# Moving operands of the two networks' products at many SBUF offsets instead of one

## The chip, the cores and the metric

The kernel runs on one core of a Trainium2 chip. Its time is the device time of one execution in microseconds (us); the figure for a kernel is the median of its runs, so lower is better. TensorE's clock has two levels, 1.2 and 2.4 GHz; the profile gives it as a share of 2.4 GHz.

## The reference, cut to what matters

Windowed attention (4 batches, 8 heads, 576 positions, head size 64) gives 2304 tokens of 512 features. Two feed-forward networks follow, one after the other, each 512 to 2048 to 512:

```python
x = attention(q, k, v)                  # 2304 x 512
h = x @ moe_w_in                        # 2304 x 2048
g = np.maximum(h, 0.0) + alpha * np.minimum(h, 0.0)
x = g @ moe_w_out                       # 2304 x 512
h = x @ moe2_w_in
g = np.where(h >= 1, h, np.where(h <= -1, 0.0, (h + 1) ** 2 / 4.0))
return g @ moe2_w_out
```

## The kernel before, in words

**Work.** Features lie on the 128 partitions, tokens along the free axis. The tokens of a network (a phase, `ph`) are cut into five token tiles, four of 512 and one of 256: in the first network the narrow one is the fourth tile, in the second the fifth. For each token tile the kernel goes through 16 blocks `f` of 128 hidden features. One step of that walk (a slot) makes a block of `h` in `f_h`, its activation in `f_g`, and the share of `y` that an earlier block gives in `f_y`; `f_y` runs two slots behind `f_h`. The order on each engine is the order in which the code issues.

**Products.** Every fp32 operand is split into a high part and a remainder, both float32r, and three products are added up: low weights by high data, high weights by low data, high by high. A slot has 4 chunks of 128 features, so 12 products in `f_h` (L344 to L346) and 12 in `f_y` (L384 to L386). Each has a 128x128 stationary operand (the weights) that it loads itself and a moving operand of 512 or 256 columns. With 10 token tiles and 16 blocks that is 3840 products, 3072 of 512 columns and 768 of 256.

**Moving operands.** `f_h` reads `xh` and `xl`, which `x_split` writes once per token tile and chunk: ScalarE copies `X` to `xh` (L317), VectorE subtracts (L318). They come from the pool `xs_p` with four buffers each, one per chunk. `f_y` reads `gh` and `gl`, which `f_g` (ScalarE, L366) and `f_cut` (VectorE, L372; GpSimd for the first token tile) write. They come from the pool `g_p` with two buffers each, which alternate with `f`.

**Where things lie.** Each of these buffers is 2048 bytes in a partition, and `PAD` is a tile of 336 floats that no instruction touches, placed between the early pools and the late ones. In the program as built `xh` begins at byte 135328, `xl` at 143520, `gh` at 219296 and `gl` at 223392, and all twelve buffers begin at 160 modulo 2048, which is 32 modulo 128. The weights' tiles (`wih`, `wil`, `woh`, `wol`) are of 2048 bytes too and also begin at 160 modulo 2048; each product loads a 512-byte chunk of one.

**Around it.** Attention of the first batch runs ahead of the networks; that of the other three is issued between the products of the first network (`attention_point`). Weights are read by DMA, rebuilt by VectorE (`w_make`), and split by ScalarE and GpSimd (`w_cut`, `wo_split`).

Of the kernel before, what the change touches and what calls it, by code (L numbers as in the profile page):

```python
# [11 lines left out]
F32R = mybir.dt.float32r  # L12
# [10 lines left out]
P = 128  # L23
# [25 lines left out]
TW = 512  # L49
WARM = 10  # L50

PAD = 336
DS = D + 1

FIRST = (0, 2)
# [24 lines left out]
def attention_then_two_ffns(ctx: ExitStack, tc: tile.TileContext, a0, aqk, av, w1i, w1o, w2i, w2o, alpha, masks, ident, out):  # L80
# [5 lines left out]
    xs_p = ctx.enter_context(tc.tile_pool(name="xs_p", bufs=4))  # L86
# [5 lines left out]

    ctx.enter_context(tc.tile_pool(name="pad", bufs=1)).tile([P, PAD], F32, name="pad")
    X = [const.tile([P, NT], F32, name=f"X{c}") for c in range(NC)]
# [216 lines left out]
    def x_split(n, c, on_pool=False):  # L311
        ph, t = n
        t0, w = TILES[ph][t]
        hi = xs_p.tile([P, TW], F32R, tag="xh", name="xh")
        lo = xs_p.tile([P, TW], F32R, tag="xl", name="xl")
        src = X[c][:, t0:t0 + w]
        nc.scalar.activation(hi[:, :w], src, AF.Copy)  # L317
        (nc.gpsimd if on_pool else nc.vector).tensor_tensor(lo[:, :w], src, hi[:, :w].bitcast(F32), ALU.subtract)  # L318
        xt[n, c] = (hi, lo)
# [28 lines left out]
    def f_g(n, f, between):  # L348
        ph, t = n
        w = TILES[ph][t][1]  # L350
        ps = ht.pop((n, f))[:, :w]
        t = g_p.tile([P, TW], F32, tag="g", name="g")[:, :w]
        hi = g_p.tile([P, TW], F32R, tag="gh", name="gh")[:, :w]
        lo = g_p.tile([P, TW], F32R, tag="gl", name="gl")[:, :w]
        if ph == 0:

            nc.scalar.activation(t, ps, AF.Relu, scale=-1.0)  # L357
            between()
            nc.vector.scalar_tensor_tensor(t, t, al[:, f:f + 1], ps, ALU.mult, ALU.add)  # L359
            ps = t  # L360
        else:
            nc.vector.tensor_scalar(t, ps, 1.0, -1.0, ALU.min, ALU.max)  # L362
            nc.scalar.activation(t, t, AF.Square, bias=half, scale=0.5)  # L363
            between()
            nc.vector.tensor_tensor(ps, ps, t, ALU.max)  # L365
        nc.scalar.activation(hi, ps, AF.Copy)  # L366
        gt[n, f] = (hi, lo)
        return ps
# [37 lines left out]
    with tc.manual_schedule(), ExitStack() as late:  # L406
# [75 lines left out]
        for i in range(NGB):  # L482
            e_scores(i)
            if i >= 1:
                a_turn(i - 1, ps_a, "a")
            e_exp(i)
            if i >= 2:
                a_out(i - 2, ps_a, "w")
            else:
                fill(2)  # L490
            if i >= 1:
                e_values(i - 1)
            w_cut()
            if i in FIRST:
                conv(3)
            if i == 3:
                x_split(n0, 0, True)

                nc.gpsimd.memset(qk[0], 0.0)
                hold = False  # L500
                a_load_qk(NGB)
                w_load(*pend_l.pop(0))
                w_load(*pend_l.pop(0))
                a_load_v(NGB)
                more()
            if i == 4:
                x_split(n0, 1, True)
# [5 lines left out]
        conv(1)  # L513
        e_values(NGB - 1)
        x_split(n0, 2)
        f_h(n0, 0, (1,))
        f_h(n0, 1, (1,))
# [17 lines left out]
        g_p = late.enter_context(tc.tile_pool(name="g_p", bufs=2))  # L535
# [25 lines left out]
        for k in range(len(slots) + 2):  # L561
            n, f = slots[k] if k < len(slots) else (None, None)
# [13 lines left out]
            if n:  # L576
                if nn and f == NF - 1:
                    for c in range(NC):
                        x_split(nn, c)
                if k < 2:  # L580
                    ops = EARLY[k]
                elif n == n0:
                    ops = 6
                elif n == order[5] or (n == order[4] and 2 <= f < NF - 2):
                    ops = 3 + 3 * (f % 2)
                else:
                    ops = 0
                attention_point()
                b0, b1 = BEFORE[n[0]]
                g = f_g(n, f, lambda: conv(min(ops, b0)))  # L590
                ops -= min(ops, b0)
                first_ops = min(ops, b1) if k else 1
                conv(first_ops)
                f_cut(n, f, g)
                if k == 0:
                    wo_split(n, f)
                w_cut()
# [97 lines left out]
```

## Time and profile before

| | |
|---|---|
| median of 3 runs | 878.41 us (877.32 to 879.67) |
| span of the profiled execution, first to last instruction | 875.2 us |
| mean granted TensorE clock | 0.994 |
| TensorE busy | 859.9 us, 98% of the span |
| VectorE, ScalarE, GpSimd busy | 53%, 43%, 32% |

The profile records only the span of its execution, not that execution's own device time; the median of the runs is 3.2 us above the span. PE is TensorE's matmul, PEld its weight load, DVE VectorE, ACT ScalarE, POOL GpSimd, SP SyncE. A matmul's end is modelled and matmuls overlap in the record, so the pace of a row of products is read from their starts.

### The profile page before, as it was taken

The page shows a single profiled execution, that of the slowest core. Times are in us where ns is not written, and L with a number is a line of the kernel's source. Part 1 is how long each engine was busy: PE and PEld are TensorE (multiplying, and loading weights), DVE is VectorE, ACT ScalarE, POOL GpSimd, SP SyncE. Part 2 cuts the span into 40 slices and gives each one's busy share as a digit, 9 for nine tenths or more (in the row PEclk, how much of TensorE's full clock was granted, in tenths as well). Part 3 has the DMA queues.
Part 4 walks back from the last instruction along what each step waited for, and adds up shares of the span by engine and source line. Part 5 has one row for each costly group of instructions (what it writes and reads, how often), then busy time and mean ns, then how long its engine had stood idle before and what let it go on. Part 6 is the DMA issues. An engine that isn't in the chain of part 4 may idle for free.

```text
span 875.2 us, 13866 instructions
## 1 busy us (share of the span) xinstructions
PE 859.9 (98%) x5472; PEld 715.7 (82%) x5474; DVE 460.8 (53%) x769; ACT 372.7 (43%) x715; POOL 276.1 (32%) x221
## 2 busy tenths in 40 slices
PE   6899999999999999999999999999999999999998
PEld 3677778888888888998888888888888888888898
DVE  4788875333543334347876994443344335433443
ACT  3444445444454334454444443433343334433454
POOL 3365543112122122444443242222222222222243
PEclk9899999999999999999999999999999999999999
DMA  7787741131121400002442320010001000000100
GB/s 293 242 246 227 204 128 40 38 76 38 49 68 38 140 1 0 1 1 79 156 147 77 121 73 1 2 47 1 1 11 38 1 1 18 31 1 1 49 1 25
DMA packets 24832, 59.34 MB, mean 68 GB/s; under 512 B 2880, under 2 KB 10688, under 8 KB 24768
## 3 DMA queue, kind: packets, MB, share of 16 engines
q1 hardware_dynamic: 24480, 58.30, 21.4%
q8 instruction: 43, 0.70, 0.3%
q14 instruction: 21, 0.17, 0.1%
q10 hardware_dynamic: 288, 0.16, 0.1%
HBM read 53.73 MB, written 4.72 MB: 67 GB/s over the span
## 4 chain that ended last, share of the span: by engine, by line
PE 93%; DVE 3%; DMA 1%; ACT 1%; SPq 1%; issue 0%; POOL 0%; ACTq 0%; DVEq 0%
PE y L384 15%; PE h_ps L344 15%; PE y L385 15%; PE y L386 15%; PE h_ps L345 15%; PE h_ps L346 15%; PE o_ps L217 2%; PE s_ps L139 1%; DMA st<-w1o 1%; PE x_ps L232 1%; PE t_ps L206 1%; DMA mask<-masks 1%; DVE wf L289 0%; SPq L262 0%; DVE w_ps L295 0%
## 5 line engine op out<-in xcount | busy, mean ns | idle before, releaser
L331 POOL TENSOR_TENSOR wol<-wo,woh 128x512 fp32r<-128x512 f32 x160 | 206.7, 1292 | 501.3 <-ACT woh L330 501.3
L344 PE MATMUL h_ps<-xh,wil 128*128 128x512 f32 (+1 forms) x640 | 239.6, 374 | 2.3 <-DVE g L359 2.0
L384 PE MATMUL y<-gh,wol 128*128 128x512 f32 (+1 forms) x640 | 237.8, 372 | 0.0
L345 PE MATMUL h_ps<-xl,wih 128*128 128x512 f32 (+1 forms) x640 | 236.5, 370 | 0.2 <-DVE xl L318 0.2
L346 PE MATMUL h_ps<-xh,wih 128*128 128x512 f32 (+1 forms) x640 | 236.3, 369 | 0.0
L385 PE MATMUL y<-gh,woh 128*128 128x512 f32 (+1 forms) x640 | 235.6, 368 | 0.0
L386 PE MATMUL y<-gl,woh 128*128 128x512 f32 (+1 forms) x640 | 235.6, 368 | 0.0
L344 PEld LDWEIGHTS h_ps<-xh,wil 128*128 128x128 f32 x640 | 121.1, 189 | 25.5 <-issue 3.6
L384 PEld LDWEIGHTS y<-gh,wol 128*128 128x128 f32 x640 | 120.7, 189 | 21.7 <-issue 1.6
L346 PEld LDWEIGHTS h_ps<-xh,wih 128*128 128x128 f32 x640 | 121.2, 189 | 20.5
L345 PEld LDWEIGHTS h_ps<-xl,wih 128*128 128x128 f32 x640 | 121.1, 189 | 19.6 <-DVE xl L318 0.5
L386 PEld LDWEIGHTS y<-gl,woh 128*128 128x128 f32 x640 | 120.7, 189 | 20.1
L385 PEld LDWEIGHTS y<-gh,woh 128*128 128x128 f32 x640 | 120.8, 189 | 19.1
L363 ACT ACTIVATE g<-g,half 128x512 f32<-128x512 f32 (+1 forms) x80 | 54.5, 681 | 145.2 <-DVE g L362 145.1
L330 ACT ACTIVATE woh<-wo 128x512 fp32r<-128x512 f32 x160 | 99.3, 622 | 12.3 <-DVE wo L289 9.4
L359 DVE SCALAR_TENSOR_TENSOR g<-g,al,h_ps 128x512 f32<-128x512 f32 (+1 forms) x80 | 55.4, 692 | 92.0 <-ACT g L357 91.8
L366 ACT ACTIVATE gh<-g 128x512 fp32r<-128x512 f32 (+1 forms) x80 | 47.1, 589 | 103.5 <-PE y L385 63.9
L362 DVE TENSOR_SCALAR g<-h_ps 128x512 f32<-128x512 f32 (+1 forms) x80 | 50.8, 635 | 67.9 <-PE h_ps L346 67.9
L365 DVE TENSOR_TENSOR h_ps<-h_ps,g 128x512 f32<-128x512 f32 (+1 forms) x80 | 51.7, 646 | 59.2 <-ACT g L363 59.2
L372 DVE TENSOR_TENSOR gl<-h_ps,gh 128x512 fp32r<-128x512 f32 (+1 forms) x80 | 50.9, 637 | 55.0 <-ACT gh L366 55.0
L372 DVE TENSOR_TENSOR gl<-g,gh 128x512 fp32r<-128x512 f32 (+1 forms) x64 | 40.0, 626 | 65.0 <-ACT gh L366 55.5
L366 ACT ACTIVATE gh<-h_ps 128x512 fp32r<-128x512 f32 (+1 forms) x80 | 44.4, 555 | 69.6 <-PE y L385 44.7
(67 smaller groups left out, 573.4 us busy)
## 6 DMA issues: line engine op xcount, KB each, us to landing
st<-w1i SPq DMA_DIRECT2D x16, 512.0 KB, 4.5
st<-w1o SPq DMA_DIRECT2D x16, 512.0 KB, 4.8
st<-w2i SPq DMA_DIRECT2D x16, 512.0 KB, 3.4
st<-w2o SPq DMA_DIRECT2D x16, 512.0 KB, 3.3
qk<-aqk SPq DMA_DIRECT2D x36, 208.0 KB, 4.1
vz<-av SPq DMA_DIRECT2D x36, 195.0 KB, 3.5
out_t<-X SPq DMA_DIRECT2D x16, 256.0 KB, 2.0
e_in<-a SPq DMA_DIRECT2D x6, 416.0 KB, 7.6
```

The source lines that it names most:

```text
L330: nc.scalar.activation(hi, wf, AF.Copy)
L331: nc.gpsimd.tensor_tensor(lo, wf, hi.bitcast(F32), ALU.subtract)
L344: nc.tensor.matmul(ps[:, :w], wl[:, cs], xh[:, :w], start=(c == 0), stop=False)
L345: nc.tensor.matmul(ps[:, :w], wh[:, cs], xl[:, :w], start=False, stop=False)
L346: nc.tensor.matmul(ps[:, :w], wh[:, cs], xh[:, :w], start=False, stop=(c == NC - 1))
L359: nc.vector.scalar_tensor_tensor(t, t, al[:, f:f + 1], ps, ALU.mult, ALU.add)
L363: nc.scalar.activation(t, t, AF.Square, bias=half, scale=0.5)
L366: nc.scalar.activation(hi, ps, AF.Copy)
L372: (nc.gpsimd if n == order[0] else nc.vector).tensor_tensor(lo, ps, hi.bitcast(F32), ALU.subtract)
L384: nc.tensor.matmul(o, wl[:, cs], gh, start=(f == 0), stop=False)
L385: nc.tensor.matmul(o, wh[:, cs], gh, start=False, stop=False)
L386: nc.tensor.matmul(o, wh[:, cs], gl, start=False, stop=(f == NF - 1))
```

## The change

`xh` and `xl` get 32 floats more per buffer (2176 bytes), so that the eight buffers begin 128 bytes further on from one to the next, modulo 2048; within its buffer the operand begins 0, 32, 64 or 96 bytes in, by token tile (`t % 4`). `gh` and `gl` are widened in the same way, and the operand begins 0 to 96 bytes in by `f // 2 % 4`. `PAD` shrinks by the 1024 bytes that `xs_p` grows, so that the late pools, with the weights of blocks 8 to 15 and the output weights' splits, stay where they were. The number of buffers, of instructions and their order are as before. Since the step between buffers is 128 bytes, every buffer still begins at 32 modulo 128.

```diff
-PAD = 336
+PAD = 80
+SLIP = 32
 DS = D + 1
@@ def x_split(n, c, on_pool=False):
-        hi = xs_p.tile([P, TW], F32R, tag="xh", name="xh")
-        lo = xs_p.tile([P, TW], F32R, tag="xl", name="xl")
+        o = 8 * (t % 4)
+        hi = xs_p.tile([P, TW + SLIP], F32R, tag="xh", name="xh")[:, o:o + TW]
+        lo = xs_p.tile([P, TW + SLIP], F32R, tag="xl", name="xl")[:, o:o + TW]
@@ def f_g(n, f, between):
-        hi = g_p.tile([P, TW], F32R, tag="gh", name="gh")[:, :w]
-        lo = g_p.tile([P, TW], F32R, tag="gl", name="gl")[:, :w]
+        o = 8 * (f // 2 % 4)
+        hi = g_p.tile([P, TW + SLIP], F32R, tag="gh", name="gh")[:, o:o + w]
+        lo = g_p.tile([P, TW + SLIP], F32R, tag="gl", name="gl")[:, o:o + w]
```

## Rows read from the trace of the kernel before

**Rows 1.** Page, parts 1 and 2: busy us and share; granted clock in 40 slices.

```profile
PE 859.9 (98%) x5472; PEld 715.7 (82%) x5474; DVE 460.8 (53%) x769; ACT 372.7 (43%) x715; POOL 276.1 (32%) x221
...
PEclk9899999999999999999999999999999999999999
```

**Rows 2.** Page, part 4: the chain that ended last, by engine and line.

```profile
PE 93%; DVE 3%; DMA 1%; ACT 1%; SPq 1%; issue 0%; POOL 0%; ACTq 0%; DVEq 0%
PE y L384 15%; PE h_ps L344 15%; PE y L385 15%; PE y L386 15%; PE h_ps L345 15%; PE h_ps L346 15%; PE o_ps L217 2%; PE s_ps L139 1%; DMA st<-w1o 1%; PE x_ps L232 1%; PE t_ps L206 1%; DMA mask<-masks 1%; DVE wf L289 0%; SPq L262 0%; DVE w_ps L295 0%
```

**Rows 3.** One line's view, L385 in 500 to 800 us: durations, first and last start.

```profile
L385 PEld LDWEIGHTS y<-gh,woh x220: 188/188/188, 501.2 to 797.0; 128*128 128x128 f32 x110
L385 PE MATMUL y<-gh,woh x220: 389/389/390, 501.4 to 797.2; 128*128 128x512 f32 x110
```

**Rows 4.** Timeline of PE, 256-column products at 372 us: start us, length us, line.

```profile
371.77 0.28 PE L344 MATMUL h_ps<-xh,wil 128*128 128x256 f32 x1
...
373.93 0.28 PE L384 MATMUL y<-gh,wol 128*128 128x256 f32 x1
```

**Rows 5.** Timeline of PE, 512-column products from 39 to 43 us.

```profile
39.28 0.68 PE L344 MATMUL h_ps<-xh,wil 128*128 128x512 f32 x1 [1.96 <-DVE g L359]
39.76 0.63 PE L345 MATMUL h_ps<-xl,wih 128*128 128x512 f32 x1
...
42.74 0.42 PE L346 MATMUL h_ps<-xh,wih 128*128 128x512 f32 x1
```

**Rows 6.** Stretches: engines' busy us (instructions), granted clock, DMA share, GB/s.

```profile
39.40:42.80 3.40, 3.40 (x9) 2.66 (x10) 2.88 (x6) 2.56 (x5) 2.92 (x3) 0.50 1.01 290
...
400.00:450.00 50.00, 50.00 (x222) 41.42 (x221) 38.41 (x58) 21.64 (x37) 22.05 (x17) 1.00 0.42 137
500.00:550.00 50.00, 50.00 (x222) 41.42 (x221) 33.88 (x53) 19.93 (x33) 16.70 (x13) 1.00 0.12 42
600.00:650.00 50.00, 50.00 (x222) 41.44 (x221) 22.02 (x32) 19.67 (x32) 11.56 (x9) 1.00 0.00 1
750.00:800.00 50.00, 50.00 (x222) 41.40 (x221) 19.43 (x28) 17.61 (x29) 12.74 (x10) 1.00 0.00 0
```

**Rows 7.** Timeline of PE, 512-column products just after attention's small ones.

```profile
207.21 0.39 PE L345 MATMUL h_ps<-xl,wih 128*128 128x512 f32 x1
...
208.37 0.39 PE L344 MATMUL h_ps<-xh,wil 128*128 128x512 f32 x1
```

**Rows 8.** Lines kept apart by shape: the activation's chain and the operands' writers.

```profile
L363 ACT ACTIVATE g<-g,half 128x512 f32<-128x512 f32 x64 | 46.3, 724 | 132.7 <-DVE g L362 132.7
L365 DVE TENSOR_TENSOR h_ps<-h_ps,g 128x512 f32<-128x512 f32 x64 | 44.8, 699 | 49.0 <-ACT g L363 49.0
L372 DVE TENSOR_TENSOR gl<-h_ps,gh 128x512 fp32r<-128x512 f32 x64 | 44.1, 690 | 46.1 <-ACT gh L366 46.1
L362 DVE TENSOR_SCALAR g<-h_ps 128x512 f32<-128x512 f32 x64 | 44.0, 688 | 63.0 <-PE h_ps L346 63.0
...
L366 ACT ACTIVATE gh<-h_ps 128x512 fp32r<-128x512 f32 x64 | 38.3, 598 | 59.9 <-PE y L385 43.4 <-DVE h_ps L365 16.5
...
L318 DVE TENSOR_TENSOR xl<-X,xh 128x512 fp32r<-128x512 f32 x30 | 24.2, 859 | 3.7 <-ACT xh L317 3.7
...
L317 ACT ACTIVATE xh<-X 128x512 fp32r<-128x512 f32 x32 | 19.2, 629 | 0.5
```

**Rows 9.** Waits over the span: us in total, times, longest.

```profile
ACT gh L366 <- PE y L385: 108.6, 89, 2.9
```

## The prediction

> **What bounds the kernel now.** I read the page's busy shares first: TensorE is busy 98% of the span, and the granted clock stands at 9 tenths or more in all but one slice [rows 1]. The chain that ended last says the same of the path: 93% is TensorE, and six lines, the networks' products, hold 15% each [rows 2]. So the question is what one product costs, and whether an operand's place is part of that cost.
>
> The second view is one line of products in a stretch that holds nothing else on TensorE [rows 3]. There are 220 rows of L385, and all have the same length to 1 ns; their weight loads have too. A slot has 24 products, four of them on L385, so 220 rows are 55 slots, and from the first to the last start lie 54 x 24 + 9 = 1305 products in 295.8 us: 226.7 ns each. For 256 columns I count starts in the timeline: 18 products in 373.93 - 371.77 = 2.16 us, 120.0 ns each [rows 4]. The second 256 columns of a wide product therefore cost 106.7 ns, 0.417 ns a column, one column per cycle at 2.4 GHz. What is left is fixed: 120.0 - 106.7 = 13.3 ns per product at either width.
>
> Third, the same products at half clock. They follow a wait of 1.96 us, the granted clock is 0.50 (1.2 GHz) [rows 5, 6], and 7 products take 42.74 - 39.76 = 2.98 us, 426 ns each. 512 columns at 1.2 GHz are 426.7 ns. So at half clock the fixed part is gone: it is not a number of the array's cycles, but something in front of or behind the array that shows only when columns go through at full rate. Feeding the moving operand could be that.
>
> Fourth, four stretches of 50 us [rows 6]. TensorE starts 222 products in each, while VectorE's busy time falls from 38.4 to 19.4 us, GpSimd's from 22.1 to 11.6 at the least, and the DMA share from 0.42 to 0.00. What others read and write in the SBUF beside a product does not change its time.
>
> **The change part by part.** All 3840 products keep their shape, weights and order. At the two prices they take 3072 x 226.7 + 768 x 120.0 = 788.6 us of the span's 875.2; the other 86.6 us (the first batch's attention, small products between, the end) have no operand that moves by design. The fixed part is 3840 x 13.3 = 51.1 us. That is all a better place could give back: the rest is one column per cycle.
>
> *The read of the moving operand.* Its start goes from one residue (160 modulo 2048) to 32 for `xh` and `xl` and 16 for `gh` and `gl`. The trace has no network product with another residue, so the price must be bounded. From below: the whole fixed part goes, -13.3 ns each, -51.1 us. From above: the nearest rows of products off their pace are those after attention's small ones, 208.37 - 207.21 = 1.16 us for 5, 232 ns, 5.3 ns over [rows 7]; as the far end I take the fixed part once more, +13.3 ns. I take 0, for three reasons. An operand of 2048 bytes passes through every residue modulo 2048 wherever it begins, so its place shifts the order in which it meets them and nothing else. The pace is even to 1 ns over buffers that lie far apart and next to any traffic [rows 3, 6], so nothing that collides by chance is in the 13.3 ns. And the fixed part is the same for 512 and 256 columns, as a turnover from one product to the next would be.
>
> On SBUF the Trainium skill says the same of traffic (SBUF — State Buffer, "Who interferes with whom"): TensorE has two read ports of its own, one for the moving operand and one for the weights, and waits on no other engine; the four stretches agree, with 222 products in each. It is silent on offsets of the kind changed here.
>
> *The writes.* 40 pairs of L317 and L318 and 160 pairs of L366 and L372 write at a multiple of 32 bytes into their buffers, in the same shapes and in contiguous runs, so I leave their durations [rows 8]. From below nothing can be gained, as none of them is on the chain [rows 2]. From above: the products that read a `gl` come two slots after its `h`, behind four batches of 12 products, 4 x 12 x 226.7 ns = 10.9 us. Before that stands the chain L362, L363, L365, L366, L372, which takes 0.69 + 0.72 + 0.70 + 0.60 + 0.69 = 3.4 us plus waits; even twice the 1.29 us of its last two fits. If this cover were gone, each slot would pay the growth: 160 x 0.1 us for a tenth of a microsecond, 16 us. I take 0.
>
> *The buffers.* There are as many as before, so ScalarE's wait for `gh` to come free (89 times, 108.6 us) stays, released by the same product [rows 9]. No queue gets or loses an instruction or a DMA, and `PAD` is touched by none.
>
> The sum is 0 us on the span of 875.2. The profile doesn't give its execution's own time; the runs' median is 3.2 us above that span, and I keep this distance: 878.4 us.
>
> **The rivals.** *The start of the operand costs, and by blocks of 128 bytes (faster).* The fixed 13.3 ns are 32 columns of 0.417 ns, that is 32 x 4 = 128 bytes of the moving operand. Every operand starts 32 bytes past a multiple of 128, so 2048 bytes touch 17 blocks of 128 bytes in place of 16, and 1024 bytes touch 9 in place of 8. If blocks were fetched whole at one column per cycle, that would make 17 x 32 = 544 columns, 226.7 ns, and 9 x 32 = 288, 120.0 ns: both figures exactly [rows 3, 4], and at half clock it could hide. For it speaks this match, and that it would be even. Against it, a plain turnover fits the same two numbers. By it the change would free only operands that begin 96 bytes further on: in `f_h` the fourth token tile of each network, 2 x 16 x 12 = 384 products; in `f_y` the blocks 6, 7, 14 and 15, 10 x 4 x 12 = 480. 864 x 13.3 ns = 11.5 us off: 866.9 us.
>
> The Trainium skill (TensorE: Matmul & The Clock Gate, "Wait — 56ns, not 53.3ns?") gives N / 2.4 GHz + 2.5 ns for products back to back and N / 1.2 GHz when cold. The cold rows here agree with it (426 ns), the warm ones do not: 226.7 ns where it has 215.8, 10.9 ns more. If the place of the operand were all of that difference and every new place were free of it, 3840 x 10.9 ns = 41.9 us would go, 836.5 us; no run here shows which.
>
> *Moving operand and weights out of step (slower).* Now both begin at 160 modulo 2048, and a weight load begins as the product before it starts. If that common phase keeps the two reads apart, other phases make them meet. It would hit the operands shifted by 32 to 96 bytes: in `f_h` three of five token tiles, 1152 products, in `f_y` three of four blocks, 1440. At 5.3 ns [rows 7] the price is 2592 x 5.3 = 13.7 us, 892.1 us; at 13.3 ns, 34.5 us. It decides from 1 ns per shifted product on (2.6 us). Against it: a moving read covers 2048 bytes in 213 ns, a weight load 512 bytes in 188 ns [rows 3], so the two drift past each other in every product whatever their starts.
>
> *Nothing moves in time though the operands move* is the forecast itself; that the operands would not move is excluded, since the offset is in the access that the products use.
>
> **How the numbers follow.** About 0.3%, 2.6 us, is what a measurement here can tell: the three runs lie 877.32 to 879.67, 0.27% apart. The forecast, no change, gets 0.71. The block rule and weaker gains from placement get 0.17: the match of 128 bytes is striking, but it is a match found after the fact. Out of step, or any loss from placement, gets 0.12. The predicted time is the likeliest case's, 878.4. Alone it would reach from 876 to 881; with 0.29 outside I extend it to the block rule, 866, and on the other side to 882, for small losses. The slower case at its price and the full gain stay out, some 0.15 together. Faster 0.17, same 0.71, slower 0.12.
>
> **What would show it.** In the changed kernel the view of L385 in a stretch of the second network should again give 389 ns for every row and 226.7 ns from start to start, in each block alike, and 222 products per 50 us. Under the block rule the timeline would show two paces: 213 ns in `f_y` of blocks 6, 7, 14, 15 and in `f_h` of the fourth token tile, 226.7 elsewhere. Out of step would show as three quarters of the `f_y` batches slower than the rest. A longer L366 or L372 with TensorE idle before L384 would be the writes. The prediction is wrong if the pace depends on the block or the token tile.

## The result, and the profile after

The changed kernel takes 890.91 us (median of 4 runs, 890.59 to 892.15) against 878.01 for the kernel before (4 runs, 877.32 to 879.67): ratio 1.0146, 95% interval 1.0132 to 1.016. It is 12.9 us slower, where no change was predicted. The profiled execution took 890.74 us, with a span of 888.9. Where both are on record, the time of this kernel and of those near it lies 1.7 to 1.9 us above the span. By that, the profiled execution of the kernel before, with its span of 875.2, was about 1 us faster than its median, which is why the spans differ by 13.7 us and the medians by 12.9.

From the page of the changed kernel, busy shares and granted clock:

```profile
PE 874.9 (98%) x5474; PEld 715.5 (80%) x5474; DVE 461.2 (52%) x769; ACT 373.0 (42%) x715; POOL 276.9 (31%) x221
...
PEclk8899999999999999999999999999999999999999
```

TensorE is busy 15.0 us longer than in [rows 1], and its weight load, VectorE, ScalarE and GpSimd are as they were. The chain is still TensorE's:

```profile
PE 96%; DVE 2%; ACT 1%; issue 1%; DVEq 0%; ACTq 0%
```

So no wait has come in; the products themselves have become slower. The view of one line in the same 300 us as [rows 3] (L388 is L385 of before):

```profile
L388 PEld LDWEIGHTS y<-gh,woh x216: 187/188/193, 501.8 to 799.3; 128*128 128x128 f32 x108
L388 PE MATMUL y<-gh,woh x216: 388/394/404, 502.0 to 799.5; 128*128 128x512 f32 x108
```

The even pace is gone: lengths run from 388 to 404 ns in place of 389 to 390. The four stretches that answer to [rows 6], with the same columns:

```profile
400.00:450.00 50.00, 50.00 (x217) 40.54 (x216) 38.13 (x59) 21.14 (x36) 20.86 (x17) 1.00 0.38 127
500.00:550.00 50.00, 50.00 (x218) 40.50 (x217) 37.18 (x58) 20.25 (x34) 16.72 (x13) 1.00 0.18 59
600.00:650.00 50.00, 50.00 (x216) 40.36 (x215) 18.68 (x27) 16.27 (x27) 11.61 (x9) 1.00 0.00 1
750.00:800.00 50.00, 50.00 (x216) 40.34 (x215) 19.95 (x29) 17.45 (x30) 11.63 (x9) 1.00 0.06 22
```

216 to 218 products per 50 us in place of 222, at the full clock, and again whatever the other engines do: the quietest stretches have the fewest. (The view counts every product that reaches into a stretch, so a count is one or two above 50 us divided by the pace.) In the narrow token tile it goes the other way (PE's timeline of the changed kernel):

```profile
380.22 0.28 PE L387 MATMUL y<-gh,wol 128*128 128x256 f32 x1
...
381.62 0.28 PE L346 MATMUL h_ps<-xh,wil 128*128 128x256 f32 x1
```

This batch of 12 products in 1.40 us took 116.7 ns each, where [rows 4] had 120.0; others took more. Over all pairs of neighbouring products that no other matmul or stop parts, the mean from start to start goes from 227.2 to 232.1 ns at 512 columns and from 119.9 to 118.5 at 256. That is 3072 x 4.9 = 15.1 us lost and 768 x 1.4 = 1.1 us won: 14.0 us, and the span grew by 13.7. The whole change lies in the pace of the products.

The writers are as they were (L375, L369, L320 and L319 are L372, L366, L318 and L317 of before, with 690, 598, 859 and 629 ns in [rows 8]):

```profile
L375 DVE TENSOR_TENSOR gl<-h_ps,gh 128x512 fp32r<-128x512 f32 x64 | 44.2, 690 | 48.8 <-ACT gh L369 48.8
...
L369 ACT ACTIVATE gh<-h_ps 128x512 fp32r<-128x512 f32 x64 | 38.3, 599 | 62.9 <-PE y L388 48.1 <-DVE h_ps L368 14.9
...
L320 DVE TENSOR_TENSOR xl<-X,xh 128x512 fp32r<-128x512 f32 x30 | 24.2, 861 | 3.7 <-ACT xh L319 3.5
...
L319 ACT ACTIVATE xh<-X 128x512 fp32r<-128x512 f32 x32 | 19.3, 627 | 0.7
```

### The profile page after: what moved, and what is told of

Read it like the earlier page. It is cut to its first block, busy times and chain, and to the rows that moved or that the text cites. A ratio compares the mean times of both kernels' runs of the same rounds, so it can differ in the third digit from the quotient of the medians.

```text
span 888.9 us, 13868 instructions
## 1 busy us (share of the span) xinstructions
PE 874.9 (98%) x5474; PEld 715.5 (80%) x5474; DVE 461.2 (52%) x769; ACT 373.0 (42%) x715; POOL 276.9 (31%) x221
## 4 chain that ended last, share of the span: by engine, by line
PE 96%; DVE 2%; ACT 1%; issue 1%; DVEq 0%; ACTq 0%
PE y L387 15%; PE h_ps L346 15%; PE y L389 15%; PE y L388 15%; PE h_ps L348 15%; PE h_ps L347 15%; PE o_ps L218 2%; PE s_ps L140 1%; PE t_ps L207 1%; PE x_ps L233 1%; PE warm_ps L448 1%; PE o_ps L200 0%; PE s_ps L176 0%; DVE wf L290 0%; DVE w_ps L296 0%
## 5 line engine op out<-in xcount | busy, mean ns | idle before, releaser
L348 PE MATMUL h_ps<-xh,wih 128*128 128x512 f32 (+1 forms) x640 | 239.0, 373 | 0.0
L388 PE MATMUL y<-gh,woh 128*128 128x512 f32 (+1 forms) x640 | 237.8, 372 | 0.0
L388 PEld LDWEIGHTS y<-gh,woh 128*128 128x128 f32 x640 | 120.5, 188 | 21.9
L366 ACT ACTIVATE g<-g,half 128x512 f32<-128x512 f32 (+1 forms) x80 | 54.5, 681 | 149.4 <-DVE g L365 149.3
L369 ACT ACTIVATE gh<-g 128x512 fp32r<-128x512 f32 (+1 forms) x80 | 47.1, 589 | 105.2 <-PE y L388 69.6
L375 DVE TENSOR_TENSOR gl<-h_ps,gh 128x512 fp32r<-128x512 f32 (+1 forms) x80 | 51.0, 637 | 57.8 <-ACT gh L369 57.8
L369 ACT ACTIVATE gh<-h_ps 128x512 fp32r<-128x512 f32 (+1 forms) x80 | 44.5, 556 | 72.7 <-PE y L388 49.5
L375 DVE TENSOR_TENSOR gl<-g,gh 128x512 fp32r<-128x512 f32 (+1 forms) x64 | 40.1, 626 | 67.2 <-ACT gh L369 57.4
```

The lines of the kernel that those rows point to most:

```text
L348: nc.tensor.matmul(ps[:, :w], wh[:, cs], xh[:, :w], start=False, stop=(c == NC - 1))
L375: (nc.gpsimd if n == order[0] else nc.vector).tensor_tensor(lo, ps, hi.bitcast(F32), ALU.subtract)
L388: nc.tensor.matmul(o, wh[:, cs], gh, start=False, stop=False)
```

## The experiments

Below, the phase of a product is the start of its moving operand minus the start of the weights that are loaded while it runs, in bytes within a partition, modulo 512 (the four chunks of a weights' tile lie 512 bytes apart). In the kernel before it is 0 in every product. All weights of a run lie at one residue modulo 256, so the product's own weights would give the same phase to within that. A pace is the mean from start to start of neighbouring products.

**All moving operands moved alike.** Two empty tiles, one ahead of `xs_p` and one ahead of `g_p`, move all moving operands, and `PAD` shrinks so that the late weights stay. For 32 bytes:

```diff
-PAD = 336
+PAD = 328
+    ctx.enter_context(tc.tile_pool(name="padx", bufs=1)).tile([P, 8], F32, name="padx")
+        late.enter_context(tc.tile_pool(name="padg", bufs=1)).tile([P, 8], F32, name="padg")
```

> All moving operands begin at one place again, 192 modulo 2048, 32 bytes further on than in the kernel before; the weights stay at 160. Theory A (the phase between the moving read and the weight load that runs beside it sets the pace): every product slower by a similar amount, near the 233.6 ns that operands at multiples of 64 bytes average in the changed kernel; span about 895 us. Theory B (the variety costs: an operand that begins at another residue than the one before it): 226.7 ns, span 875 us as before. Theory C (the absolute residue of the moving operand costs): slower as in A.

Measured: 894.32 us (before, on the same chip, 876.77), span 892.5. The timeline of its PE shows 269 products from the first to the second row:

```profile
498.87 0.40 PE L385 MATMUL y<-gh,wol 128*128 128x512 f32 x1
...
561.64 0.39 PE L387 MATMUL y<-gl,woh 128*128 128x512 f32 x1
```

62.77 us / 269 = 233.3 ns; the narrow tiles run at 116.8. One place for all operands and no variety at all, and it is slower than the changed kernel. So a loss needs no variety (theory B).

The same with 32 floats in place of 8, 128 bytes:

> All moving operands at 288 modulo 2048, 128 bytes further on, weights at 160. Theory A: an even pace other than 226.7 ns, near the 231 ns that operands at 32 modulo 64 average in the changed kernel, span about 888 us; if only the place within 128 bytes counts, 226.7 ns and 875 us. Theory B: 226.7 ns, 875 us. Theory C: as A.

892.70 us, span 890.9, 232.5 ns. The place within 128 bytes is the old one, so that is not what counts.

**Weights and moving operands moved together.** One empty tile ahead of the weights' first pool moves everything behind it by 32 bytes:

```diff
+    ctx.enter_context(tc.tile_pool(name="padw", bufs=1)).tile([P, 8], F32, name="padw")
     wp = ctx.enter_context(tc.tile_pool(name="wp", bufs=1))
```

> Weights and moving operands both at 192 modulo 2048, so that their phase is that of the kernel before. Theory A and theory B: 226.7 ns, span 875 us. Theory C: as slow as the run with the moving operands alone at 192, about 895 us.

The even pace is back, in the same 300 us:

```profile
L386 PE MATMUL y<-gh,woh x222: 389/389/389, 499.9 to 799.8; 128*128 128x512 f32 x111
```

The moving operands lie where they lay in the first run, at 192 modulo 2048, and run at 226.7 ns: their own residue (theory C) is not the cause. The one execution took 879.67 us (before 876.77) with a span of 877.9; the 2.6 us over the span of before lie ahead of the second token tile, whose first product starts at 138.5 us against 135.9, and from there on the tiles take the same times.

**The weights moved instead.** Weights at 640 modulo 2048, moving operands at 672, that is at their old residue modulo 512:

```diff
-PAD = 336
+PAD = 328
+    ctx.enter_context(tc.tile_pool(name="padw", bufs=1)).tile([P, 120], F32, name="padw")
+    ctx.enter_context(tc.tile_pool(name="padx", bufs=1)).tile([P, 8], F32, name="padx")
+        late.enter_context(tc.tile_pool(name="padg", bufs=1)).tile([P, 8], F32, name="padg")
```

> The weights are moved instead: they lie at 640 modulo 2048 and all moving operands at 672, which is where they were modulo 512; the phase is 32 bytes as in the run with all moving operands 32 further on. Theory A, phase to the weights modulo 512: 233.3 ns for 512 columns, 116.7 for 256, span near 892 us, the same as that run. Rival, the moving operand's phase to something else than the weights (X, or its own residue modulo 512, which is as before): 226.7 and 120.0 ns, 875 us.

895.06 us (before 877.15), 233.3 and 116.8 ns, and 216 products per 50 us:

```profile
600.00:650.00 50.00, 50.00 (x216) 40.22 (x215) 18.75 (x27) 16.54 (x27) 11.23 (x10) 1.00 0.00 1
```

Same phase, same pace, whichever side was moved. These four runs settle the cause: it is the phase between the moving operand and the weights (theory A). Each is one execution, but the three at another phase are 16 to 18 us above the kernel before, whose executions spread over less than 4 us.

**Steps by buffer alone.** The changed kernel with both offsets at 0, so that only the 128-byte steps are left:

```diff
-        o = 8 * (t % 4)
+        o = 0
-        o = 8 * (f // 2 % 4)
+        o = 0
```

> The 128-byte steps by buffer alone, no offset by token tile or block. Theory A: the phase differs by multiples of 128 bytes, so near 231 ns on average, span about 885 us, and 228 to 235 ns by buffer. Theory B: about as slow as the changed kernel, 889 us, since neighbours still differ. If only the place within 128 bytes counts: 875 us.

888.50 us, span 886.7, and 269 products in 62.16 us, 231.1 ns:

```profile
495.74 0.39 PE L387 MATMUL y<-gh,wol 128*128 128x512 f32 x1
...
557.90 0.40 PE L389 MATMUL y<-gl,woh 128*128 128x512 f32 x1
```

11.5 of the 13.7 us are there with no offset inside a buffer. Half of the wide products are at phase 0 or 256, half at 128 or 384. In kernels that keep to one phase these have 226.8 and 232.5 ns (table below), 229.7 on average; the 1.4 ns on top come with the mixture. So a loss needs no variety, but this mixture costs more than its phases do one by one.

**Other phases.** The same empty tiles with other sizes, one phase for `f_h` and another for `f_y`; in the narrow token tiles, which fill half of a buffer, the operand is moved inside it.

```diff
+        o = OX[ph] if w < TW else 0
-        hi = xs_p.tile([P, TW], F32R, tag="xh", name="xh")
+        hi = xs_p.tile([P, TW], F32R, tag="xh", name="xh")[:, o:o + w]
```

> f_h's moving operands 64 bytes past the weights' residue, f_y's 96 (512 columns); in the two token tiles of 256 columns the phases are 64 and 96 in the first network, 16 and 48 in the second. If the phase to the weights sets the pace batch by batch (theory A): f_h near 230 ns and f_y near 234 ns, the averages of operands at those phases in the changed kernel, and 256 columns under 120 ns, as all phases but 0 gave so far. Rival, the pace is a state that carries over from batch to batch: both batches at one common pace.

890.12 us; `f_h` 229.7 ns, `f_y` 233.3 ns; narrow 117.8 and 119.9, then 115.5 and 118.0.

> Phases 256 in f_h and 384 in f_y; 256-column tiles at 256 and 384, then 160 and 192. Theory A with a period of 512 bytes: both near 231 ns, slower than before. If the period were 256 bytes: f_h at 226.7 ns; if 128, both, but 128 was slow already.

886.41 us; `f_h` 228.2 ns in the first network and 228.0 in the second, `f_y` 232.7; narrow 118.8 and 119.0, then 118.1 and 116.1.

> Phases 480 (that is 32 bytes short of the weights' residue) in f_h and 192 in f_y; 256-column tiles at 480 and 448, then 320 and 224. Theory A: f_h near 233 ns, f_y near 232, by the averages in the changed kernel; one phase in it (xl of the second chunk at 192) ran at 226 ns, so f_y could also be as fast as before. None below 226 ns is expected.

892.86 us; `f_h` 232.8 ns, `f_y` 233.1; narrow 118.3 and 117.7, then 116.2 and 118.4. Each batch has a pace of its own, none at 512 columns below 226.7. But it isn't given by the batch's own phase alone: `f_h` at phase 64 takes 229.7 ns in the first of these three runs, with `f_y` at 96, and 228.9 below, with both at 64.

**Scans that told little.** To give each token tile a phase of its own, all buffers of `xh` and `xl` were made one tile, and those of `gh` and `gl` another (`o = f % 2 * TW + OG[n]` and so on). In one tile, the code's order makes `f_y` of a block stand behind the write of the block two later into the same place, so nearly all shares of `y` come from the wrong block; the instructions are the same.

> The buffers of xh and xl are one tile, and those of gh and gl another, so that each token tile can have its own phase to the weights in all of its products: in the eight 512-column tiles 0, 4, 8, 16, 24, 496, 504 and 508 bytes in f_h and 0, 12, 20, 40, 48, 80, 320 and 448 in f_y; in the two narrow ones 4 and 8, and 12 and 496. Theory A with phase 0 as the best place: 226.7 ns at 0 alone, 228 to 234 at the others; the narrow ones below 120 ns. Rival, the fixed 13.3 ns are themselves a meeting of the two reads, which some phase avoids: at one of them 213 to 220 ns at 512 columns.

> The same with 112, 144, 160, 176, 208, 240, 272 and 304 bytes in f_h and 224, 256, 288, 320, 352, 416, 448 and 464 in f_y; narrow tiles 24 and 304, and 112 and 272. Theory A with phase 0 as the best place: 228 to 234 ns everywhere, 256 near the 228.4 of its own run; narrow tiles 115 to 120 ns. Rival as in the fine scan: somewhere 213 to 220 ns.

1606.33 and 1604.34 us. TensorE therefore waited for the newer block's operand in nearly every one of the 160 slots. The waits of the first of the two (us in total, times, longest):

```profile
PE y L387 <- ACT gs L369: 433.4, 148, 7.0
```

The mean granted clock fell to 0.83. Phase 0 stands only in `f_h` of the first token tile and reads 230.6 ns there, where the kernel before has 229.6. No phase averaged below 230 ns at 512 columns, but these runs can't place one.

**Scans with separate buffers.** Buffers of 2560 bytes, so that all begin at the same residue modulo 512, and one staging buffer fewer to make room:

```diff
-NST = 5
+NST = 4
+SLIP = 128
-PAD = 336
+PAD = 208
-        hi = xs_p.tile([P, TW], F32R, tag="xh", name="xh")
+        o = OX[n]
+        hi = xs_p.tile([P, TW + SLIP], F32R, tag="xh", name="xh")[:, o:o + w]
```

> Buffers of 2560 bytes, all at the weights' residue modulo 512, one staging buffer for weights fewer to make room, and each token tile with one phase in all its products: 24, 48, 8, 96 bytes in the first network's wide tiles, 0, 16, 64, 192 in the second's, 8 and 64 in the narrow ones. If the order of buffers mattered, 0 would not give 226.7 ns here. Theory that phase 0 is the best place for 512 columns: 226.7 ns at 0, 229 to 235 at the others. Rival, the fixed 13.3 ns are themselves a meeting of the two reads that some phase avoids: 213 to 220 ns at one of them. Narrow tiles below 120 ns.

> The same with 480, 384, 448 and 4 bytes in the first network's wide tiles, 256, 320, 496 and 504 in the second's, 256 and 496 in the narrow ones. Phase 0 the best place: 228 ns at 256, 230 to 235 at the others, 4 and 504 included if any step off 0 costs, or 226.7 there if only whole lines of 16 bytes count. Rival: 213 to 220 ns at one of them.

889.91 and 894.00 us. PE's timeline of the first, tiles with phase 0 and with phase 64, 269 products from the first to the second row of each pair:

```profile
498.56 0.39 PE L389 MATMUL y<-gh,wol 128*128 128x512 f32 x1
...
559.56 0.39 PE L391 MATMUL y<-gl,woh 128*128 128x512 f32 x1
...
674.77 0.39 PE L389 MATMUL y<-gh,wol 128*128 128x512 f32 x1
...
736.34 0.39 PE L391 MATMUL y<-gl,woh 128*128 128x512 f32 x1
```

and of the second, phases 256 and 320:

```profile
500.83 0.39 PE L389 MATMUL y<-gh,wol 128*128 128x512 f32 x1
...
561.86 0.39 PE L391 MATMUL y<-gl,woh 128*128 128x512 f32 x1
...
588.21 0.39 PE L389 MATMUL y<-gh,wol 128*128 128x512 f32 x1
...
649.78 0.39 PE L391 MATMUL y<-gl,woh 128*128 128x512 f32 x1
```

61.00 and 61.03 us / 269 are 226.8 and 226.9 ns; 61.57 and 61.57 are 228.9 and 228.9. Phases 256 apart have the same pace. All paces of token tiles in which `f_h` and `f_y` have one phase, worked out in this way from the runs above and the three at the end of this section (in the first network, where attention comes between, without the twelve products after it; the first token tile, with phases 24 and 480 in the two scans, is left out):

| phase, bytes | 512 columns, ns | 256 columns, ns |
|---|---|---|
| 0 | 226.8 | 119.9 |
| 4 | 236.7 | |
| 8 | 233.3 | 117.0 |
| 16 | 231.7 | 118.7 |
| 32 | 233.3 | 116.8 |
| 48 | 233.3 | |
| 64 | 228.9 | 117.8 |
| 96 | 233.3 | |
| 128 | 232.5 | 118.7 |
| 192 | 233.2 | 117.8 |
| 256 | 226.9 | 119.9 |
| 320 | 228.9 | 117.8 |
| 384 | 232.6 | |
| 448 | 233.3 | |
| 496 | 236.7 | 117.2 |
| 504 | 233.3 | |

Phase 0 (and 256) is the fastest of those tried at 512 columns, by 2 to 10 ns, and the slowest at 256 columns, by 1 to 3.

**The spread in steps of 256.** If the period is 256 bytes, many offsets cost nothing as long as they differ by multiples of it. The changed kernel with other steps:

```diff
-PAD = 80
-SLIP = 32
+PAD = 16
+SLIP = 64
-        o = 8 * (t % 4)
+        o = 64 * (t % 2)
-        o = 8 * (f // 2 % 4)
+        o = 64 * (f // 2 % 2)
```

> The changed kernel with every step made a multiple of 256 bytes: buffers 2304 bytes apart, the operand 0 or 256 bytes in by token tile and by block, so that the twelve buffers' operands lie at all eight multiples of 256 modulo 2048 from the weights' residue. If the pace depends on the phase to the weights modulo 256 bytes alone: 226.7 and 120.0 ns, span 875 us, ratio 1.000. Rival, that a spread over many offsets costs by itself or that the period is longer: 229 ns or more, ratio 1.008 or more.

878.45 us against 878.32, ratio 1.000 (0.999 to 1.0009), and the even pace in the view of its line:

```profile
L388 PE MATMUL y<-gh,woh x222: 389/389/389, 499.8 to 799.7; 128*128 128x512 f32 x111
```

**Narrow tiles off phase, wide tiles on it.** The kernel before, with only the two narrow token tiles' operands moved inside their buffers (`OX` and `OG` as above, no empty tiles).

> The kernel before, with the operands of the two 256-column token tiles alone begun 16 bytes further on inside their buffers; the eight 512-column tiles stay at phase 0. Theory A: 512 columns keep 226.7 ns; 256 columns go from 120.0 to about 115.5 ns as in the first network's f_h at that phase, 768 products x 4.5 ns = 3.5 us off, near 874.7 us, ratio 0.996. Rival, the gain at 256 columns belongs to a kernel whose wide tiles are off phase too: 120.0 ns and no change.

> The same with the narrow tiles at phase 192 in the first network and 320 in the second. Theory A: about 116.1 ns in both, 768 x 3.9 = 3.0 us off, ratio 0.997. Rival: no change.

> The kernel before with the two narrow token tiles alone at phase 32. The run with all moving operands 32 further on had 116.7 ns there: 768 x 3.2 ns = 2.5 us off, ratio 0.997, if a phase's pace is its own; 120.0 ns and no change if not.

| kernel | median, us | ratio, 95% interval | 256 columns, ns |
|---|---|---|---|
| phase 16 | 876.50 | 0.9981 (0.9972 to 0.9990) | 118.7 |
| phases 192, 320 | 876.06 | 0.9977 (0.9968 to 0.9987) | 117.8 |
| phase 32 | 875.59 | 0.9973 (0.9964 to 0.9981) | 116.7 |

All three are faster than both kernels, by little but clear of the noise. At phase 32 PE's timeline has 18 products in 368.58 - 366.48 = 2.10 us:

```profile
366.48 0.28 PE L388 MATMUL y<-gh,wol 128*128 128x256 f32 x1
...
368.58 0.28 PE L347 MATMUL h_ps<-xh,wil 128*128 128x256 f32 x1
```

768 x 3.2 ns = 2.5 us were expected there, and 2.7 us came (878.32 to 875.59). The other two fell short. At phase 16 the pace was 118.7 ns and not 115.5, and 1.6 us came in place of 3.5 (878.13 to 876.50); at 192 and 320 it was 117.8 and not 116.1, and 2.1 us came in place of 3.0 (878.13 to 876.06). The 115.5 had been measured with `f_y` at phase 48, and the paces near 116 with the other batch at 160 or 224: a pace measured in a mixture didn't carry over to one phase throughout.

## Why the prediction was wrong

**What bounds the kernel** held: the products set the time, at 13.3 ns above one column per cycle, and the whole change lies in their pace. **The writes** and **the buffers** at 0 held too. ScalarE's wait for a free `gh` grew from 108.6 [rows 9] to 119.0 us, as is to be expected where the products that release it come later. The 3.2 us kept between span and median were in part a fast profiled execution (the distance is 1.8 us); the forecast's time is the median of before either way.

**The step that failed is the read of the moving operand, "I take 0".** Measured are +4.9 ns per wide product on average and -1.4 per narrow one. Of its three reasons:

- "its place shifts the order in which it meets them and nothing else": the place against the weights is what counts. With every operand at one new place the pace is 233.3 ns; with the weights moved as well it is 226.7 again.
- "nothing that collides by chance is in the 13.3 ns": true, and no argument. An even pace shows that whatever happens happens in the same way each time, and in the kernel before the phase was the same in every product. All twelve operand buffers and all weights lay at one residue, so that trace could say nothing about another; I took a sample of one phase for evidence on all.
- "the fixed part is the same for 512 and 256 columns", as a turnover would be: of the phases tried, only at 0 and 256. At phase 32 the two widths have 20.0 and 10.1 ns above one column per cycle.

**The slower rival had the mechanism**, with 0.12, and its 892.1 us lies near the 890.9 measured; but the sum behind that figure is not what happened. It charged 2592 products whose place within 128 bytes changes with 5.3 ns each. In fact steps of 128 bytes alone, which it charged nothing, cost 11.5 us of span; wide products pay 4.9 ns on average, those at phase 0 among them (230.0 ns), and narrow ones gain. That the two figures lie close is luck. What spoke against it, that two reads of different speed drift past each other whatever their starts, does not hold: a start 4 bytes off costs 10 ns per product (236.7).

**The block rule fell.** In the run with `f_y` at phase 96 its operands begin at 256 modulo 2048, a multiple of 128, and take 233.3 ns, not 213.3. The match of 13.3 ns with 128 bytes did not hold at another place.

**The pages weighed.** By the Trainium skill's TensorE: Matmul & The Clock Gate ("Wait — 56ns, not 53.3ns?") the surplus of a warm product is 2.5 ns; at none of the phases tried is a batch that near on average, and the least are 13.3 ns at 512 columns and 8.8 at 256 (115.5 ns). By the Trainium skill's SBUF — State Buffer ("Who interferes with whom") the ports for moving operand and weights are independent; here the pace of one depends on where the other lies. The measurements decide. On other engines' traffic nothing here speaks against the page: the two stretches of the changed kernel with the least work on VectorE have the fewest products, 216.

**What stays open** is what in the chip meets with a period of 256 bytes, and why 0 is best at 512 columns and worst at 256. The runs show that the phase decides and what each costs where all products have it, not where the time is spent. In a mixture a product's pace also hangs on its neighbours, and no run gives a rule for that: `xl` at phase 192 takes 225.9 ns on average in the changed kernel, and 233.2 where all products are at 192. Whether it is the weights being loaded or the product's own that count can't be told, as all lie at one residue modulo 256. The phases between those of the table weren't tried on their own.

## What to carry to other kernels

Where TensorE is the bound and float32r products load their own weights, as here, the place of the moving operand against the weights is a parameter of the kernel, worth up to 4% of a product's time: for 512 columns keep the two a multiple of 256 bytes apart, and measure other shapes. Measure a phase with all products at it, for a pace from a mixture may not carry over. A constant pace in a trace shows only that a cost is regular; whether it depends on a quantity can't be read from a trace in which that quantity never varies. And where a change spreads many things at once, the run that tells most is the one that moves them all alike, and then the other side with them.

## What the runs showed of the hardware that was not expected

- The pace of float32r products that each load 128 columns of weights, all at one phase, depends on the moving operand's start minus the weights' start, with a period of 256 bytes: 226.8 to 236.7 ns at 512 columns and 116.8 to 119.9 ns at 256, at the full clock. A step of 4 bytes is enough (236.7 ns).
- The two widths want different places: the phase that is best at 512 columns, 0, is the worst of those tried at 256.
- The pace is held over from batch to batch: `f_h` at phase 256 took 228.0 ns with `f_y` at 384 in the second network (its first three products 231 to 232 ns, the other nine 226.7), and 226.9 with `f_y` at 256; narrow `f_h` at 16 took 115.5 ns with `f_y` at 48, and 118.7 with it at 16.
